# An S4 convolution and gMLP kernel on one core: constant matmuls put into the opening of TensorE's stream

## The chip, the core and the metric

The kernel runs on one core of one Trainium2 chip. A core has five engines with instruction streams of their own: TensorE (matmuls out of SBUF into PSUM; its weight loads are shown as a stream of their own, PEld), VectorE (DVE), ScalarE (ACT), GpSimd (POOL) and SyncE (SP, which here only starts transfers). The metric is the device time in microseconds, as a median over runs; lower is better.

## What is computed

One block with two halves, each behind a layer norm whose shift and scale come from a conditioning vector. The first half is a diagonal state space model with complex poles, applied as a long convolution over 2048 positions; the second is a gated MLP with a 2048 × 2048 matrix over positions. All inputs and outputs are float32.

```
mod = (silu(c) @ w_mod) -> sa, ca, ga, sb, cb, gb          # 576 -> 6 x 576
h = layernorm(x) * (1 + ca) + sa
  dt = exp(log_dt);  P = exp(dt * A * l), l = 0..2047
  K = real(sum_n C * P * dt * B)                            # 576 x 2048, 128 poles a channel
  y = irfft(rfft(h) * rfft(K)) + h * Dskip
x = x + ga * y
h = layernorm(x) * (1 + cb) + sb
  z = gelu(h @ w_in);  z1, z2 = halves;  z2 = layernorm(z2)
  g = w_sp @ z2 + b_sp
x = x + gb * ((z1 * g) @ w_out)
```

## The kernel before

The change lies in the function `ssm`, which does the first half; the MLP, which takes the greater part of the time, is not touched.

The order of the work in `ssm` is written out by hand. `ORDER` is a long string of steps; each is a letter and a number, and the letter names a generator function. At each mention of a step the generator runs on to its next `yield`, so the pieces of one unit are spread between those of others. Every instruction is pinned: each engine executes its instructions in the order in which the program issues them, and waits in place for what an instruction needs. Buffers in SBUF and PSUM are taken from rings whose order is written out too (`PLAN`); in PSUM `pk` has four banks of 512 float32 columns and `ps` two pairs of banks.

The steps that the change or the prediction touches:

- `O` and `P` (`poles`): VectorE and ScalarE turn the poles' inputs into exponents and phases, split each into three bfloat16 parts and store them in DRAM (through POOL's queue). `O` is for the first quarter of the channels, `P` for the rest.
- `M0` to `M5` (`mod_unit`): one sixth of w_mod each. TensorE multiplies the six row chunks of a half (288 columns) by silu(c) (`ec`), four chunks side by side in 32 array columns each, into bank `pm[0]` for the first half and `pm[1]` for the second. ScalarE copies both into `mpart`; the step's next piece sums the four row groups with a matmul by `ones` ("row sum") into two further banks. M2 comes first (it gives `gar`, the gate), then M1 (`cga`), M0 (`sga`), and later M3 to M5. M2's products are the first work of TensorE in the program.
- `e` (`e_unit`), `t` (`t_unit`), `p` (`p_unit`): for each of 36 groups of channels the poles' exponentials (ScalarE) and their sines and cosines, from phases that TensorE makes by bfloat16 products with selection matrices (`sel`), and the products of both (VectorE).
- `k` (`kg_unit`, the pole unit): contracts over the 128 poles on TensorE, in small tiles, into the first 256 columns of one bank; ScalarE copies them to `kab`.
- `1` (`k1_unit`): the first stage of the transform of the filter, from `kab` into the first 256 columns of two banks.
- `S`, `R`, `A` (`ln_stats`, `ln_rows`, `ln_half`): the layer norm, and the first stage of the transform of the rows, sixteen `A` units of two row blocks and 288 channels each, into four banks, 64 partitions for each block.
- `u`, `z`, `v`, `y`: the further stages of the transform, the multiplication in the frequency domain, and the way back.

`small` is a tile of constants in SBUF, 7 × 128 float32 columns; `eye`, its first 128 columns, is the unit matrix. `halfpi` is a column of the tile `consts_s`, which VectorE fills at the program's start; `bc(ap, shape)` broadcasts a column without a copy. `HC` is 288. The products of M, of the row sums and of the A units fill 288 of 512 columns, those of the k and 1 units 256.

The helper that records every instruction is line 224, so nearly all rows of the profile have this line; they are told apart by tiles.

Of the kernel before, what the change touches and what calls it, by code (L numbers as in the profile page):

```python
# [48 lines left out]
    "zz": "01011010010100010110100110101101010101",  # L49
}  # L50
ON_ACT = set()
PE_SUMS = set(range(28, 36))
PE_ADDS = set(range(8, 20))
ORDER = """
# [182 lines left out]
def ssm(tc, I, x1_d, consts_s, dram, mod_d, mlp):  # L237
# [3 lines left out]
    HC = 288  # L241
    ring = Rings()
    CW = 16 * 9 * 128
    with ExitStack() as ctx:
# [10 lines left out]
        def ps2():  # L255
            return ring(psp, [128, 2, 512], F32, "ps", 2)

        def ps1():
            return ring(psp, [128, 512], F32, "pk", 4)
# [175 lines left out]
        gsp = ep.tile([128, D], BF, name="gsp", bufs=1)  # L435
        msk = cp.tile([128, 2], F32, name="msk")

        def mod_unit(k):
            wm = wmt.pop(k)
            pm = [ps1(), ps1()]  # L440
            for hh in range(2):
                for kt in range(6):
                    j = (kt + 2 * hh) % 4
                    T.matmul(pm[hh][32 * j:32 * j + 32, :HC], ec[:, kt:kt + 1].to_broadcast([96, 32]),
                             wm[hh][:, kt], start=kt < 4, stop=kt >= 2, skip_group_check=True)
            yield
            mpart = ep.tile([128, D], F32, name="mpart", bufs=1)
            for hh in range(2):
                A.activation(v3(mpart)[:, hh], pm[hh][:, :HC], AF.Copy)
            yield  # L450
            pm = [ps1(), ps1()]
            for hh in range(2):
                T.matmul(pm[hh][:, :HC], ones, mpart[:, HC * hh:HC * hh + HC], start=True, stop=True)
            yield
            src = [t[:, :HC] for t in pm]
            if k == 2:
                for hh in range(2):
                    A.activation(v3(gar)[:, hh], src[hh], AF.Copy)
            elif k == 1:
                for hh in range(2):  # L460
                    V.scalar_tensor_tensor(v3(cga)[:, hh], src[hh], 1.0, v3(gar)[:, hh], op0=ALU.add, op1=ALU.mult)
            elif k == 0:
                for hh in range(2):
                    V.tensor_tensor(v3(sga)[:, hh], src[hh], v3(gar)[:, hh], op=ALU.mult)
                yield
                for i in range(2):
                    A.activation(gsp, sga, AF.Copy)
                    yield
                    V.scalar_tensor_tensor(sga, gsp, msk[:, i:i + 1], sga, op0=ALU.mult, op1=ALU.add)
                    yield  # L470
                A.activation(gsp, sga, AF.Copy)
            else:
                mrow = mpart if k == 4 else ep.tile([128, D], F32, name="gar", bufs=1)
                for hh in range(2):
                    if k == 4:
                        A.activation(v3(mrow)[:, hh], src[hh], AF.Identity, bias=one)
                    else:
                        A.activation(v3(mrow)[:, hh], src[hh], AF.Copy)
                yield
                G.dma_start(mod_d[k - 3:k - 2], mrow[0:1])  # L480
# [59 lines left out]
        def ln_half(k):  # L540
            p, h = divmod(k, 2)
            c = slice(HC * h, HC * h + HC)
            pms = [ps1() for _ in range(4)]
            for t in range(2):
                n, rt, cs = row[2 * p + t]
                for x, y, st in ((cs, gsp, True), (rt, n, False)):
                    for g in range(4):
                        rows = slice(32 * g, 32 * g + 32)
                        T.matmul(pms[g][64 * t:64 * t + 64, :HC], x[rows], y[rows, c], start=st, stop=not st, skip_group_check=True)
                yield  # L550
            o = ring(ep, [128, 4, HC], F32, "st1o", 2)
            for g, pm in enumerate(pms):
                A.activation(o[:, g], pm[:, :HC], AF.Copy)
                yield
            G.dma_start(u1_d[:, 2 * p:2 * p + 2, :, :, c].rearrange("g b r k d -> (b r k) g d"), o)
# [22 lines left out]
        def t_unit(g):  # L578
            c, gi = divmod(g, 9)
            pa = ps2()  # L580

            def phases(cols, start, stop):
                for k, (n, c0) in enumerate(zip(("lc", "la"), cols)):
                    for h, (l, r) in enumerate(zip(halves(lt[n, c], gi), rows(c0, 256))):
                        T.matmul(pa[:, h].rearrange("p (c k j) -> p k c j", c=8, k=2)[:, k], l, r, start=start, stop=stop, skip_group_check=True)

            def magics(c0, start):
                for h, (l, r) in enumerate(zip(rows(c0, 128), rows(2048, 64))):
                    T.matmul(pa[:, h].rearrange("p (c j) -> p c j", c=8), l, r[:, None, :].to_broadcast([48, 8, 64]), start=start, stop=False,
                             skip_group_check=True)  # L590

            if g in ROUNDED:
                magics(2112, True)
                phases((768, 0), False, False)
                magics(2240, False)
                phases((1536, 1792), False, True)
                yield
                cs = tt[g] = ring(tb, [128, 2, 2, 512], F32, "ft", 3)
                ct, f = cs[:, 0], cs[:, 1]
                if g in ON_ACT:  # L600
                    A.activation(ct, pa, AF.Abs)
                else:
                    V.tensor_single_scalar(ct.bitcast(I32), pa.bitcast(I32), 0x7FFFFFFF, op=ALU.bitwise_and)
                yield
                A.activation(f, pa, AF.Sin, scale=-TWO_PI)
            else:
                phases((768, 0), True, True)
                yield
                cs = tt[g] = ring(tb, [128, 2, 2, 512], F32, "ft", 3)
                ct, f = cs[:, 0], cs[:, 1]  # L610
                A.activation(f, pa, AF.Copy, bias=MAGIC)
                yield
                V.scalar_tensor_tensor(f, f, MAGIC, pa, op0=ALU.subtract, op1=ALU.subtract)
                yield
                V.tensor_single_scalar(ct.bitcast(I32), f.bitcast(I32), 0x7FFFFFFF, op=ALU.bitwise_and)
                yield
                A.activation(f, f, AF.Sin, scale=-TWO_PI)
            yield
            A.activation(ct, ct, AF.Sin, bias=halfpi, scale=-TWO_PI)
# [17 lines left out]
        def kg_unit(g):  # L637
            pr, pi, gr, gi = tt.pop(g)
            pm = ps1()
            for j in range(4):  # L640
                rows = slice(32 * j, 32 * j + 32)
                T.matmul(pm[rows, 63:256:64], eye[:, rows], dsk[:, 4 * g:4 * g + 4], start=True, stop=False, skip_group_check=True)
            for i in range(4):
                for x_, y_, sp in ((gr, pr, False), (gi, pi, True)):
                    for j in range(4):
                        c = 8 * (j // 2) + 2 * i + j % 2
                        T.matmul(pm[32 * j:32 * j + 32, 64 * i:64 * i + 64], x_[:, c], y_[:, c].rearrange("p s j -> p (s j)"),
                                 start=False, stop=sp, skip_group_check=True)
            yield
            kk = kab[g] = ring(tb, [128, 4, 64], F32, "kab", 2)  # L650
            A.activation(kk, pm[:, :256].rearrange("p (i b) -> p i b", i=4), AF.Copy)

        def k1_unit(g):
            c, gi = divmod(g, 8)
            kk = kab.pop(g)
            pm = [ps1(), ps1()]
            for i in range(4):
                for ri in range(2):
                    for h in range(2):
                        s = slice(64 * h, 64 * h + 64)  # L660
                        T.matmul(pm[h][64 * ri:64 * ri + 64, 64 * i:64 * i + 64], kk[s, i], r1[ri][s, s], start=True, stop=True,
                                 skip_group_check=True)
            yield
            if c not in k1t:
                k1t[c] = ring(kp, [128, 32, 128], F32, "k1", 2)
            o = k1t[c][:, :, 16 * gi:16 * gi + 16].rearrange("p k (h c) -> p k h c", h=2)
            for h in range(2):
                pk = pm[h][:, :256].rearrange("p (c k) -> p k c", c=8)
                if (g, h) in COPIED:
                    V.tensor_copy(o[:, :, h], pk)  # L670
                else:
                    A.activation(o[:, :, h], pk, AF.Copy)
                yield
# [1794 lines left out]
```

## Time and profile before

| | |
|---|---|
| median of 3 runs | 1692.17 us (1691.11 to 1693.82) |
| the profiled execution | 1691.0 us, its span 1688.9 us |
| TensorE busy | 1615.6 us, 16868 matmuls |
| VectorE, ScalarE, GpSimd busy | 1298.4, 873.8, 209.7 us |
| mean granted TensorE clock | 0.99 |
| first matmul | 25.77 us after the span's start |

A page of the profile gives busy times by engine, the span in 40 slices, the DMA queues, the chain of work that ended last, and groups of instructions. A row of the timeline starts with the time and the duration in microseconds, then the engine, the operation, "out<-in", the shapes (for a matmul the array's rows*columns, then the moving operand) and the number of merged records (x12); in brackets stand the idle time of the engine before it and what ended this. A row of busy times gives the stretch, its length, busy time and number of instructions of each engine, the granted TensorE clock (1.00 is full), the DMA engines' busy share and GB/s. A row of waits gives who waited for whom, the sum in microseconds, the number of waits and the longest.

### The profile page before, as it was taken

To read this page: it belongs to the slowest core of one execution; us is meant where nothing else is said; L and a number is where in the kernel's file an instruction comes from. 1 tells how busy PE (TensorE), PEld (TensorE's weight loads), DVE (VectorE), ACT (ScalarE), POOL (GpSimd) and SP (SyncE) were. 2 spreads that over 40 slices of the span, in tenths; PEclk is the share of its full clock that TensorE was granted. 3 is DMA by queue.
4 is the path that set the end of the run, shared out by engine and by line. 5 is a ranking of instruction groups with operands and counts; after the bars stand their busy time and mean duration, and the time that the engine had idled before them with its cause. 6 is when DMAs were issued, how large, how long until landed. Compare 5 with 4: busy or idle time off the path is not lost.

```text
span 1688.9 us, 39922 instructions
## 1 busy us (share of the span) xinstructions
PE 1615.6 (96%) x16868; PEld 1235.7 (73%) x16868; DVE 1298.4 (77%) x2241; ACT 873.8 (52%) x1307; POOL 209.7 (12%) x340
## 2 busy tenths in 40 slices
PE   3778999989999999999999999999999999999999
PEld 1344677755555557778878888888888888888887
DVE  7898999867989877988997776894443487787555
ACT  6889999675776664555444433342321133353221
POOL 3251111112222110000000000000111100111100
PEclk9978999999999999999999999999999999999999
DMA  9667645596888898776738887664667573777560
GB/s 231 170 215 229 203 140 176 171 317 208 280 287 243 251 261 297 242 270 234 249 118 302 282 292 257 219 218 166 232 213 243 189 221 121 275 281 252 189 241 29
DMA packets 186402, 380.61 MB, mean 225 GB/s; under 512 B 38464, under 2 KB 105792, under 8 KB 185456
## 3 DMA queue, kind: packets, MB, share of 16 engines
q1 hardware_dynamic: 145216, 182.10, 35.2%
q0 software_dynamic: 34528, 169.11, 30.1%
q10 hardware_dynamic: 6480, 26.86, 3.9%
q8 instruction: 132, 2.16, 0.5%
q14 instruction: 46, 0.38, 0.1%
HBM read 272.73 MB, written 105.29 MB: 224 GB/s over the span
## 4 chain that ended last, share of the span: by engine, by line
PE 77%; DVE 7%; DMA 3%; issue 2%; ACT 2%; SPq 0%; POOL 0%; ACTq 0%; DVEq 0%; POOLq 0%
PE ps L224 58%; PE pz L224 10%; PE pk_b L224 2%; PE pk_a L224 2%; DMA zset<-set_d 2%; PE pk_c L224 2%; PE pk_d L224 1%; DVE zset L224 1%; DVE gt L224 1%; DVE bsz L224 1%; PE ps_a L224 0%; PE ps_b L224 0%; DMA v_d<-v_a 0%; PE pt L224 0%; DMA uu_a<-in_x 0%
## 5 line engine op out<-in xcount | busy, mean ns | idle before, releaser
L224 PEld LDWEIGHTS <-zset 128*128 128x128 f16 x7182 | 702.2, 98 | 86.5 <-DMA zset<-set_d 2.0
L224 PE MATMUL ps<-wsp,zset 128*128 128x256 f16 x6048 | 666.8, 273 | 2.2 <-DMA zset<-set_d 1.1
L224 PE MATMUL pz<-wz,nt 128*128 128x512 f16 (+1 forms) x1120 | 220.8, 358 | 1.5 <-ACT nt L224 1.0
L224 ACT ACTIVATE z<-gt 128x1024 f16<-128x1024 f32 x56 | 59.0, 1054 | 250.4 <-DVE gt L224 250.4
L224 PEld LDWEIGHTS <-nt 128*128 128x128 f16 x1120 | 109.4, 98 | 107.1 <-ACT nt L224 1.5
L2164 POOL DMA_DIRECT2D zset<-set_d x96 | 50.8, 529 | 862.5 <-PE ps L224 619.7
L224 PE MATMUL ps<-wout,z 128*128 128x288 f16 x1092 | 138.4, 286 | 0.0
L224 DVE SCALAR_TENSOR_TENSOR gt<-ps,sc,bsp 128x512 f32<-128x512 f32 x36 | 27.0, 749 | 143.0 <-PE ps L224 141.3
L224 PEld LDWEIGHTS <-z 128*128 128x128 f16 x1176 | 115.1, 98 | 28.9
L224 DVE TENSOR_TENSOR raw<-raw 128x256 f32<-128x256 f32 (+3 forms) x238 | 126.8, 539 | 7.7 <-DMA raw<-z_d 3.5
L224 PE MATMUL ps<-n2o,zset 128*128 128x256 f16 x1134 | 128.2, 273 | 0.0
L224 DVE SCALAR_TENSOR_TENSOR gt<-ps,sc,gt 128x512 f32<-128x512 f32 (+1 forms) x180 | 122.2, 696 | 7.6
L224 ACT ACTIVATE zset<-raw 128x1792 f16<-128x1792 f32 x48 | 81.1, 1691 | 59.3 <-PE ps L224 21.6
L224 DVE TENSOR_TENSOR zset<-raw,zset 128x1792 f16<-128x1792 f32 x48 | 96.9, 2020 | 15.7 <-ACT zset L224 15.7
L224 DVE TENSOR_TENSOR z<-ps,z 128x512 f32<-128x512 f32 (+1 forms) x126 | 72.0, 599 | 32.3 <-ACT z L224 25.9
L224 ACT ACTIVATE z<-pz,sc 128x512 f32<-128x512 f32 (+1 forms) x96 | 51.9, 574 | 39.9 <-PE pz L224 32.7
L224 ACT ACTIVATE wsp<-raw,sc 128x1792 f16<-128x1792 f32 x25 | 44.5, 1783 | 46.2 <-DVE raw L224 40.2
L224 ACT ACTIVATE z<-z,sc 128x1024 f32<-128x1024 f32 x21 | 24.1, 1148 | 76.0 <-DVE z L224 72.3
L224 ACT ACTIVATE z1b<-gt 128x512 f16<-128x512 f32 (+1 forms) x22 | 17.7, 821 | 84.0 <-DVE gt L224 84.0
L224 PE MATMUL ps<-n2q,wf 128*128 128x512 f16 x252 | 55.7, 379 | 0.0
L224 DVE BATCH_NORM_STATS2 bsz<-z 128x6 f32<-128x384 f32 x96 | 48.4, 548 | 5.0 <-ACT z L224 4.4
L224 DVE SCALAR_TENSOR_TENSOR wsp<-raw,sc,wsp 128x1792 f16<-128x1792 f32 x25 | 52.0, 2078 | 0.3 <-ACT wsp L224 0.3
(793 smaller groups left out, 2772.0 us busy)
## 6 DMA issues: line engine op xcount, KB each, us to landing
zset<-set_d POOLq DMA_DIRECT2D x96, 896.0 KB, 5.2
raw<-z_d SPq DMA_DIRECT2D x48, 512.0 KB, 5.6
set_d<-zset ACTq DMA_DIRECT2D x24, 896.0 KB, 6.4
z_d<-z POOLq DMA_DIRECT2D x32, 576.0 KB, 8.2
zset<-wa_d POOLq DMA_DIRECT2D x18, 896.0 KB, 4.9
raw<-in_w_spT SPq DMA_DIRECT2D x25, 512.0 KB, 4.4
set_d<-zset SPq DMA_DIRECT2D x12, 896.0 KB, 5.8
wst<-in_w_in SPq DMA_DIRECT2D x8, 1024.0 KB, 9.3
```

What stands on the lines that cost most here:

```text
L224: return self.tc.keep_in_program_order(f(*a, **k))
L2164: self.nc.gpsimd.dma_start(o, self.set_d[f, j - 1] if j else self.wa_d[f])
```

## The change

A new helper `warm(t, n, c0, const)` issues n float32 matmuls into the columns of the PSUM tile t from c0 to the bank's end, which no instruction reads. Their weights are the unit matrix and their moving operand columns of `small` (or, for M2, the constant column `halfpi`, broadcast to both). It is called

- in `mod_unit` ahead of the first half's products and again between the halves, with the two numbers that `WARM_M` gives for each of the six steps, and three times behind the row sums;
- in `ln_half` three times behind the second row block;
- in `t_unit` eight times ahead of the phases of group 1, over all 512 columns;
- in `kg_unit` three times behind groups 0 to 9, and in `k1_unit` three times behind groups 0 to 8.

```
@@ -49,6 +49,7 @@
     "zz": "01011010010100010110100110101101010101",
 }
 ON_ACT = set()
+WARM_M = {0: (5, 10), 1: (12, 14), 2: (116, 8), 3: (0, 3), 4: (0, 3), 5: (0, 3)}
 PE_SUMS = set(range(28, 36))
 PE_ADDS = set(range(8, 20))
 ORDER = """
@@ -435,10 +436,20 @@
         gsp = ep.tile([128, D], BF, name="gsp", bufs=1)
         msk = cp.tile([128, 2], F32, name="msk")
 
+        wide = small.rearrange("p i c -> p (i c)")
+
+        def warm(t, n, c0, const=None):
+            for _ in range(n):
+                l, r = (eye, wide[:, c0:]) if const is None else (bc(const, [128, 128]), bc(const, [128, 512 - c0]))
+                T.matmul(t[:, c0:], l, r[:, :512 - c0], start=True, stop=True, skip_group_check=True)
+
         def mod_unit(k):
             wm = wmt.pop(k)
             pm = [ps1(), ps1()]
+            warm(pm[0], WARM_M[k][0], HC, halfpi if k == 2 else None)
             for hh in range(2):
+                if hh:
+                    warm(pm[0], WARM_M[k][1], HC, halfpi if k == 2 else None)
                 for kt in range(6):
                     j = (kt + 2 * hh) % 4
                     T.matmul(pm[hh][32 * j:32 * j + 32, :HC], ec[:, kt:kt + 1].to_broadcast([96, 32]),
@@ -451,6 +462,7 @@
             pm = [ps1(), ps1()]
             for hh in range(2):
                 T.matmul(pm[hh][:, :HC], ones, mpart[:, HC * hh:HC * hh + HC], start=True, stop=True)
+            warm(pm[1], 3, HC)
             yield
             src = [t[:, :HC] for t in pm]
             if k == 2:
@@ -547,6 +559,8 @@
                     for g in range(4):
                         rows = slice(32 * g, 32 * g + 32)
                         T.matmul(pms[g][64 * t:64 * t + 64, :HC], x[rows], y[rows, c], start=st, stop=not st, skip_group_check=True)
+                if t:
+                    warm(pms[3], 3, HC)
                 yield
             o = ring(ep, [128, 4, HC], F32, "st1o", 2)
             for g, pm in enumerate(pms):
@@ -578,6 +592,8 @@
         def t_unit(g):
             c, gi = divmod(g, 9)
             pa = ps2()
+            if g == 1:
+                warm(pa[:, 0], 8, 0)
 
             def phases(cols, start, stop):
                 for k, (n, c0) in enumerate(zip(("lc", "la"), cols)):
@@ -646,6 +662,7 @@
                         c = 8 * (j // 2) + 2 * i + j % 2
                         T.matmul(pm[32 * j:32 * j + 32, 64 * i:64 * i + 64], x_[:, c], y_[:, c].rearrange("p s j -> p (s j)"),
                                  start=False, stop=sp, skip_group_check=True)
+            warm(pm, 3 if g < 10 else 0, 256)
             yield
             kk = kab[g] = ring(tb, [128, 4, 64], F32, "kab", 2)
             A.activation(kk, pm[:, :256].rearrange("p (i b) -> p i b", i=4), AF.Copy)
@@ -660,6 +677,7 @@
                         s = slice(64 * h, 64 * h + 64)
                         T.matmul(pm[h][64 * ri:64 * ri + 64, 64 * i:64 * i + 64], kk[s, i], r1[ri][s, s], start=True, stop=True,
                                  skip_group_check=True)
+            warm(pm[1], 3 if g < 9 else 0, 256)
             yield
             if c not in k1t:
                 k1t[c] = ring(kp, [128, 32, 128], F32, "k1", 2)
```

More of the change, by code (lines that the diff above doesn't have):

```diff
@@ L51 @@
 ON_ACT = set()
+WARM_M = {0: (5, 10), 1: (12, 14), 2: (116, 8), 3: (0, 3), 4: (0, 3), 5: (0, 3)}
 PE_SUMS = set(range(28, 36))
@@ L436, in ssm, with warm @@
         msk = cp.tile([128, 2], F32, name="msk")
+        wide = small.rearrange("p i c -> p (i c)")
+        def warm(t, n, c0, const=None):
+            for _ in range(n):
+                l, r = (eye, wide[:, c0:]) if const is None else (bc(const, [128, 128]), bc(const, [128, 512 - c0]))
+                T.matmul(t[:, c0:], l, r[:, :512 - c0], start=True, stop=True, skip_group_check=True)
         def mod_unit(k):
@@ L440, in mod_unit @@
             pm = [ps1(), ps1()]
+            warm(pm[0], WARM_M[k][0], HC, halfpi if k == 2 else None)
             for hh in range(2):
+                if hh:
+                    warm(pm[0], WARM_M[k][1], HC, halfpi if k == 2 else None)
                 for kt in range(6):
@@ L453, in mod_unit @@
                 T.matmul(pm[hh][:, :HC], ones, mpart[:, HC * hh:HC * hh + HC], start=True, stop=True)
+            warm(pm[1], 3, HC)
             yield
@@ L549, in ln_half @@
                         T.matmul(pms[g][64 * t:64 * t + 64, :HC], x[rows], y[rows, c], start=st, stop=not st, skip_group_check=True)
+                if t:
+                    warm(pms[3], 3, HC)
                 yield
@@ L580, in t_unit @@
             pa = ps2()
+            if g == 1:
+                warm(pa[:, 0], 8, 0)
             def phases(cols, start, stop):
@@ L648, in kg_unit @@
                                  start=False, stop=sp, skip_group_check=True)
+            warm(pm, 3 if g < 10 else 0, 256)
             yield
@@ L662, in k1_unit @@
                                  skip_group_check=True)
+            warm(pm[1], 3 if g < 9 else 0, 256)
             yield
```

## The prediction

> **What bounds the kernel now.** I read the page first (engines, slices, chain), then busy times by stretch, then the instructions of the opening in order of time.
>
> ```profile
> PE 1615.6 (96%) x16868; PEld 1235.7 (73%) x16868; DVE 1298.4 (77%) x2241; ACT 873.8 (52%) x1307; POOL 209.7 (12%) x340
> PE   3778999989999999999999999999999999999999
> PEclk9978999999999999999999999999999999999999
> PE 77%; DVE 7%; DMA 3%; issue 2%; ACT 2%; SPq 0%; POOL 0%; ACTq 0%; DVEq 0%; POOLq 0%
> ```
>
> TensorE (PE) is busy 1615.6 of 1688.9 us and makes up 77% of the chain that ended last; only the first four slices (42 us each) leave it room, and only there is the clock row below 9. So the account is TensorE's: everything put into its stream has to find a hole, and the holes are early. The stretches say how large they are.
>
> ```profile
> core 0: us, PE busy (x) PEld busy (x) DVE busy (x) ACT busy (x) POOL busy (x), PEclk, DMA share, GB/s
> 0.00:160.00 160.00, 106.90 (x1944) 54.30 (x1946) 134.67 (x276) 134.10 (x258) 57.91 (x96) 0.89 0.73 209
> 160.00:400.00 240.00, 226.30 (x4512) 162.07 (x4508) 208.36 (x305) 197.97 (x340) 41.65 (x66) 1.00 0.70 206
> 400.00:1688.90 1288.90, 1282.40 (x10419) 1019.34 (x10416) 955.41 (x1662) 541.71 (x710) 110.17 (x178) 1.00 0.70 231
> ...
> 25.70:50.60 24.90, 21.64 (x108) 8.26 (x111) 16.38 (x33) 16.55 (x25) 7.83 (x15) 1.00 1.02 256
> ...
> 77.90:84.70 6.80, 5.70 (x64) 2.65 (x71) 6.77 (x12) 6.79 (x15) 0.97 (x2) 0.50 0.55 188
> ...
> 88.50:94.50 6.00, 5.76 (x134) 3.67 (x133) 5.61 (x11) 5.40 (x10) 4.69 (x8) 0.50 0.90 320
> ...
> 98.60:108.70 10.10, 7.73 (x138) 3.95 (x134) 8.23 (x20) 8.96 (x18) 5.28 (x9) 0.51 0.72 215
> ...
> 139.60:149.80 10.20, 8.44 (x96) 3.21 (x94) 7.48 (x11) 9.16 (x17) 2.81 (x4) 0.52 0.39 141
> ```
>
> The columns after the times are busy us (and instructions) of each engine, the granted clock, the DMA share and GB/s. After 160 us TensorE idles 240 − 226.3 + 1288.9 − 1282.4 = 20.2 us in all, so nothing that is late at 160 us is made good later. Before 160 us it idles 53.1 us, 25.8 of them before its first instruction. Four stretches ran at half clock. A fifth did too, though its clock column says 1.00 (no change of clock had been recorded yet): the same group of products takes 2.13 us at 25.77 and 0.92 us at 51.99, the same sum 1.12 us (37.67 to 38.79) and 0.58 us (54.17 to 54.75).
>
> ```profile
> 25.77 2.13 PE L224 MATMUL pk_a<-wm,ec 96*32 96x288 f32 x12 [25.77 <-DVE t_q L224]
> ...
> 37.67 1.33 PE L224 MATMUL pk_a<-mpart,small 128*128 128x288 f32 x2
> 38.79 1.17 PE L224 MATMUL pk_b<-mpart,small 128*128 128x288 f32 x2
> ...
> 51.99 0.92 PE L224 MATMUL pk_c<-wm,ec 96*32 96x288 f32 x10
> ...
> 54.17 0.65 PE L224 MATMUL pk_b<-mpart,small 128*128 128x288 f32 x2
> 54.75 0.39 PE L224 MATMUL ps_b<-sel,lb 48*128 48x512 bf16 x2
> ```
>
> **The change, part by part.** Nothing is removed or moved; TensorE gets matmuls whose results nobody reads ("fillers"), all f32, 128 rows by 128 columns of weights. I count them from the diff. With 224 moving columns: M0 15, M1 26, M2 124, M3 to M5 9, the six row sums 18, sixteen row units (A) 48: together 240. With 256: ten pole units (k) 30 and nine k1 units (1) 27: 57. With 512: the second phase unit (t1) 8.
>
> *Price of one.* An f32 matmul is two records: one half of a w_mod group is six matmuls in the code and x12 in the row at 25.77, and one row sum is one matmul and x2. How long a record holds the array when equal ones follow each other stands in the v units' rows.
>
> ```profile
> 170.75 0.19 PEld L224 LDWEIGHTS pk_d<-zz_a,small 64*128 64x128 f32 x1
> 170.75 0.38 PE L224 MATMUL pk_d<-zz_a,small 64*128 64x256 f32 x1
> 170.97 0.37 PE L224 MATMUL pk_d<-zz_a,small 64*128 64x256 f32 x1
> 171.19 0.38 PE L224 MATMUL pk_d<-zz_a,small 64*128 64x256 f32 x1
> 171.40 0.38 PE L224 MATMUL pk_d<-zz_a,small 64*128 64x256 f32 x1
> ...
> L224 PEld LDWEIGHTS pk_b<-xb_b,small x2: 186/188/189, 327.3 to 327.4; 128*128 128x128 f32 x2
> ...
> 327.31 1.13 PE L224 MATMUL pk_b<-xb_b,small 128*128 128x512 f32 x2
> 328.36 0.32 PE L224 MATMUL pk_b<-u_b,st 128*64 128x128 f32 x1
> ```
>
> From 170.75 to 171.40 three steps take 0.65 us: 0.217 us for 256 columns, 0.85 ns a column, weight loads hidden. For 224 columns that is 0.19 us, just the 0.188 us that a load of 128 f32 columns takes, so 0.38 to 0.39 us a filler in a long run. Where a group stands alone, its first load shows: the 512-column matmul takes 1.05 us (327.31 to 328.36) against 2 × 512 × 0.85 ns = 0.87, the row sum 0.58 against 0.49. So each of the 51 groups gets 0.15 us on top. Sum: 240 × 0.39 = 93.6; 57 × 2 × 0.217 = 24.7; 8 × 0.87 = 7.0; 51 × 0.15 = 7.6; together 133 us. Lower end: 0.38 and no edges, 123 us. Upper end: the row sum's 0.58 us scaled by columns (0.45, 0.52, and 1.05 for the wide ones), 108 + 29.6 + 8.4 = 146 us. I take 133, because 116 of the fillers stand in one run, as the v rows do.
>
> *The front run of M2.* M2's products are TensorE's first work, and wait until 25.77 us; the fillers before them read only a constant that VectorE sets in the first microsecond.
>
> ```profile
> 0.82 0.06 DVE L185 MEMSET consts_s<- 128x1 f32 x1 [0.82 <-PEq L2457]
> ...
> PE pk_a L224 <- DVE t_q L224: 25.8, 1, 25.8
> ...
> 27.94 0.41 ACT L224 ACTIVATE mpart<-pk_a 128x288 f32<-128x288 f32 x1 [1.63 <-PE pk_a L224]
> ...
> DVE ft_c L224 <- PE ps_a L224: 4.5, 1, 4.5
> ```
>
> They start at 0.95 us and 116 × 0.39 = 45.2 us follow, some of it at half clock. From a low clock to a high one the trace shows stretches with 5.70 us (77.9) to 21.64 us (25.7) of work; half of that is lost: 2.9 to 10.8 us. The fillers are dense, so I take 2.9. M2's products then begin at 0.95 + 45.2 + 2.9 = 49 us instead of 25.77. The hole takes in 25 us; the other 24 are on the path. Late next is ScalarE: its mpart copy, 27.94 now, comes after 49, and the exponentials and splits of the poles that follow it on ScalarE wait, and VectorE for those. POOL's stores of these splits are late with them.
>
> The Trainium skill ("TensorE: Matmul & The Clock Gate", section "The HAM clock gate") says that the clock rises after about 3.4 us of sustained work and falls after an idle window of that length. By it the front run would lose 1.7 us and not 2.9, an estimate, and the total would be 1 us lower. The trace agrees only in part: the stretch at 25.7 stayed slow for 24.9 us with 21.64 us busy, at 96- and 48-row matmuls between 128-row ones.
>
> *What the clock gives back.*
>
> ```profile
> 50.60:77.90 27.30, 20.36 (x414) 10.34 (x407) 26.65 (x52) 26.42 (x54) 8.73 (x14) 1.00 0.52 129
> ...
> 108.70:139.60 30.90, 23.00 (x634) 13.48 (x624) 30.06 (x56) 28.33 (x56) 13.17 (x21) 0.99 0.73 237
> ```
>
> The five slow stretches hold 21.64 + 5.70 + 5.76 + 7.73 + 8.44 = 49.3 us of TensorE work; at full clock 24.6 us less. Bounds: zero (they stay slow) to 24.6. I take 23: with fillers behind nearly every unit the array hardly rests, and these two stretches kept the clock with the array busy three quarters of the time.
>
> *Idle time.* From 25.77 to 160 us TensorE idles 160 − 25.8 − 106.9 = 27.3 us, in short pieces; the largest sum of one kind after the first wait is this:
>
> ```profile
> PE pk_a L224 <- ACT st1o_b L224: 2.4, 2, 1.8
> ```
>
> Fillers stand where these pieces are, and the work of VectorE and ScalarE (134.7 and 134.1 us) has more time than before. I leave 6 of it (0 to 27.3).
>
> *The copies behind a filler.* ScalarE's copies of a unit's PSUM tile may have to wait for the three fillers on the same bank (0 to 1.3 us each). While TensorE is the bound this is hidden by TensorE's own next units; without that cover it lengthens the k–1 chain and the row units, 35 copies by 1.3, 46 us, and is not added to the same time twice.
>
> *Sum.* The point at which 160 us stood comes to 0.95 + 2.9 + (106.9 − 23) + 133 + 6 = 226.8 us, 66.8 later. What follows is full and stays as it is. The profiled execution took 1691.0 us for a span of 1688.9 (2.1 around it): 1688.9 + 66.8 + 2.1 = 1757.8. The median shown is 1.2 us above that execution, a spread that counts for nothing here; I say 1758.
>
> **The rivals.**
> 1. *A filler costs half.* If a constant product were one record (0.19 us), or the two ran side by side, the front run would end at 0.95 + 22.6 + 2.9 = 26.5, right where M2 waits now, and the total would be about 67 us: 0.95 + 2.9 + 83.9 + 67 + 6 = 160.8, 1693 us. It decides at 66 us of added TensorE time in all: below that the regained clock wins and the kernel is faster; with no idle left, 154.8, 1687 us. For it: the whole hole before M2 would be filled exactly. Against it: every f32 matmul with 128 weight columns in the trace has its two records, and the pitch of 0.217 us is per record.
> 2. *Loads not hidden.* With full 128-row weights a load may not go under the matmul of the same rows; the 512-column matmul showed 0.18 us for its two. At 0.39 + 0.18 = 0.57 us: 240 × 0.57 + 57 × 0.61 + 8 × 1.05 = 180 us, and the kernel comes to 1688.9 + 2.1 + 0.95 + 2.9 + 83.9 + 180 + 6 − 160 = 1805 us. Against it: v's 64-row loads, 0.19 us each, hide completely.
> 3. *The clock stays low.* If the dense f32 stream does not raise the clock sooner than the first stretch did, 10.8 us are lost in place of 2.9, and if only half of the 23 comes back, 12 more: 1778 us. For it: 21.64 us of work were needed once.
> 4. *The lateness is made good.* The 20.2 us of idle time after 160 us are used up, because VectorE and ScalarE are ahead by then: 1738 us. Against it: 8.9 us of them lie in 340 to 400, where VectorE is idle too and so not what TensorE waits for:
>
> ```profile
> 340.00:360.00 20.00, 16.69 (x202) 13.54 (x198) 14.45 (x34) 14.74 (x25) 3.29 (x6) 1.00 1.08 335
> 360.00:380.00 20.00, 16.07 (x146) 8.96 (x144) 13.79 (x34) 12.81 (x16) 4.26 (x7) 1.00 1.08 300
> 380.00:400.00 20.00, 18.32 (x129) 9.97 (x129) 9.89 (x22) 8.37 (x16) 6.31 (x9) 1.00 0.78 235
> ```
>
> **How the numbers follow.** Main case 0.68, with its own range 1740 to 1785 (123 us, idle 0 and all 24.6 back at the low end, 146 us and idle 20 at the high end); rival 1 0.08; rival 2 0.11; rival 3 0.08; rival 4 0.05. The range 1732 to 1800 takes in the main case, 3 and 4, and leaves out 1 and most of 2: 0.81. Two tenths of a per cent (3.4 us; the runs shown spread over 2.7) is what a measurement can tell from no change. Of rival 1, 0.04 ends faster, 0.03 within and 0.01 slower; everything else is slower: 0.93.
>
> **What would show it.** Right: first product of M2 near 49 us; fillers in pairs of records, 0.19 us apart; the granted clock full from some 5 us to 230; TensorE busy about 1615.6 + 133 + 3 − 23 = 1729 us; VectorE waiting 20 us or more for ScalarE or TensorE between 28 and 60; the part from u, z and v units on unchanged in length. Wrong: M2 still near 26 us (rival 1), records 0.28 us apart (rival 2), filler durations twice as long after the first 6 us (rival 3). A step of the sum that could fail unseen is the 6 us of idle time, if the units then wait for each other in turn.

## The result, and the profile after

The changed kernel takes 1760.14 us (median of 6 runs, 1753.82 to 1761.28) beside 1693.38 us of the kernel before (6 runs, 1691.11 to 1698.82): a ratio of 1.038 by the record's estimate, 95% interval 1.0362 to 1.0397 (the quotient of the two medians is 1.0394). The profiled execution took 1757.55 us for a span of 1755.6, 66.7 us more than the span before. The kernel is slower, by about the amount forecast (1758); two of the prediction's readings behind that number did not hold, and the experiments show which.

The page of the changed kernel, the lines that answer to those shown of before:

```profile
PE 1729.4 (99%) x17478; PEld 1344.0 (77%) x17478; DVE 1299.6 (74%) x2241; ACT 875.8 (50%) x1307; POOL 210.4 (12%) x340
PE   9999999998999999999999999999999999999999
PEclk9999999999999999999999999999999999999999
PE 83%; DVE 7%; DMA 4%; ACT 3%; issue 2%; POOL 0%; ACTq 0%; SPq 0%; DVEq 0%; POOLq 0%
```

TensorE has 610 matmul records more, two for each of the 305 fillers, and is busy 113.8 us longer. Its first slices are full now, and the clock row shows no slice below 9. The other engines do what they did before.

The start of TensorE's stream, from the timeline of the changed kernel:

```profile
0.94 47.10 PE L225 MATMUL pk_a<-consts_s 128*128 128x224 f32 x232 [0.94 <-DVE consts_s L188]
47.97 1.16 PE L225 MATMUL pk_a<-wm,ec 96*32 96x288 f32 x12
49.06 3.32 PE L225 MATMUL pk_a<-consts_s 128*128 128x224 f32 x16
...
66.03 4.70 PE L225 MATMUL pk_c<-small 128*128 128x224 f32 x24
```

The front run of 116 fillers (232 records) lasts 47.03 us, so M2's first products begin at 47.97 us and not at 25.77. They take 1.16 us there and not 2.13: the array is at full speed by then. The second group shows the pitch of a run: its 24 records start 0.189 us apart, 0.38 us a filler.

Busy times of the changed kernel in 10-us stretches of the front run (columns as in the prediction):

```profile
0.00:10.00 10.00, 9.06 (x34) 8.56 (x35) 6.30 (x27) 4.12 (x7) 0.21 (x4) 1.00 0.65 169
10.00:20.00 10.00, 10.00 (x55) 9.92 (x54) 6.71 (x26) 8.73 (x22) 5.41 (x9) 1.00 0.99 308
...
40.00:50.00 10.00, 10.00 (x60) 8.96 (x59) 0.00 (x0) 0.00 (x0) 0.00 (x0) 1.00 0.54 173
```

The first row holds 34 records and the second 55 (one that reaches into two stretches counts in both). The single records start 0.373 us apart up to 6 us and 0.191 us apart after that. At the later pace the 232 would take 44.3 us, so 2.7 us of the 47.03 were lost to a slow start of some 5.2 us. The clock column says 1.00 in that row too, as it did in the prediction's slow first stretch, and is not to be trusted there. In a second execution of the same kernel (after_again, below) the pace changes at 3.7 us already, M2 starts at 46.83 us, and 1.6 us are lost; over all the runs that have a front run it changes between 3.7 and 6.7 us. The Trainium skill ("TensorE: Matmul & The Clock Gate", section "The HAM clock gate") gives about 3.4 us of sustained work until the clock rises; the prediction's estimate from it, 1.7 us lost, is too low for the first execution and fits the second.

From 40 to 50 us neither VectorE nor ScalarE did anything at all. The waits of the changed kernel up to 235 us name what they waited for:

```profile
ACT mpart L225 <- PE pk_a L225: 33.7, 3, 26.9
...
DVE ft_a L225 <- PE ps_a L225: 28.7, 2, 28.1
```

The fillers alone, by groups, in the first 230 us (busy us, then mean ns of one record, then idle time before them); shown are those of M2 and the four groups with 256 columns, which are those of the k and 1 units:

```profile
L225 PE MATMUL pk_a<-consts_s 128*128 128x224 f32 x248 | 50.4, 366 | 0.9 <-DVE consts_s L188 0.9
...
L225 PE MATMUL pk_a<-small 128*128 128x256 f32 x42 | 10.9, 396 | 0.0
L225 PE MATMUL pk_d<-small 128*128 128x256 f32 x36 | 9.4, 396 | 0.0
...
L225 PE MATMUL pk_b<-small 128*128 128x256 f32 x24 | 6.2, 396 | 0.0
...
L225 PE MATMUL pk_c<-small 128*128 128x256 f32 x12 | 3.1, 396 | 0.0
```

All ten groups, 610 records, add up to 139 us. The means of 366 and 396 ns are the length of one record from its start to its modelled end; successive records overlap, and the pitch is half of that. The groups also overlap with each other and with the work records beside them: up to the mark named below the fillers' records cover 137 us, and without them TensorE would be busy 130 us less.

To see when the delay arises, the opening needs a mark that both kernels have: ScalarE's first copy `uu_a`, which opens the stages behind the fillers. For the kernel before, then for the changed one:

```profile
L224 ACT ACTIVATE uu_a<-pk_d x3: 597/598/613, 159.4 to 313.0; 128x512 f32<-128x512 f32 x3
```

```profile
L225 ACT ACTIVATE uu_a<-pk_d x3: 597/597/654, 221.2 to 373.5; 128x512 f32<-128x512 f32 x3
```

It comes 61.8 us later (159.4 to 221.2). The busy times up to this mark give the whole account; the kernel before, then the changed one:

```profile
0.00:159.40 159.40, 106.30 (x1940) 53.96 (x1940) 134.07 (x275) 133.50 (x257) 57.91 (x96) 0.89 0.73 208
```

```profile
0.00:221.20 221.20, 215.93 (x2544) 160.05 (x2544) 135.49 (x276) 134.72 (x258) 57.98 (x96) 0.99 0.53 154
```

TensorE's idle time fell from 53.1 to 5.3 us, of which 0.94 lie ahead of its first record. Its busy time rose by 109.6 us: 130 of fillers, less 20 by which its other records cover less at the higher clock (106.3 us before, 86.1 now). If time in which a filler and another record overlap is counted as the filler's, it is 137 less 28. 109.6 − 47.8 = 61.8.

The remaining 5 us of the 66.7 come behind the openings, in the MLP. From `uu_a<-pk_b` (381.4 us before, 441.9 after) to the end of the span it is 1307.5 us before and 1313.7 after; between the two copies 1.3 us were won. The rows of the long products in the kernel before and the changed one, cut to that part:

```profile
L224 PE MATMUL ps<-wsp,zset 128*128 128x256 f16 x6048 | 666.8, 273 | 2.2 <-DMA zset<-set_d 1.1 <-DVE zset L224 0.9
```

```profile
L225 PE MATMUL ps<-wsp,zset 128*128 128x256 f16 x6048 | 668.9, 273 | 6.6 <-DMA zset<-set_d 3.8 <-DVE zset L225 2.7
```

TensorE waits 4.4 us longer for `zset`, for its transfers and for VectorE. In another profile of the changed kernel the same part took 1312.4 us, in one experiment (noK) 1312.3, in all others 1307 to 1309. So it isn't one odd execution; what makes these transfers late stays open.

### The profile page after: what moved, and what is told of

Read it like the earlier page. It is cut to its first block, busy times and chain, and to the rows that moved or that the text cites. A ratio compares the mean times of both kernels' runs of the same rounds, so it can differ in the third digit from the quotient of the medians.

```text
span 1755.6 us, 41142 instructions
## 1 busy us (share of the span) xinstructions
PE 1729.4 (99%) x17478; PEld 1344.0 (77%) x17478; DVE 1299.6 (74%) x2241; ACT 875.8 (50%) x1307; POOL 210.4 (12%) x340
## 4 chain that ended last, share of the span: by engine, by line
PE 83%; DVE 7%; DMA 4%; ACT 3%; issue 2%; POOL 0%; ACTq 0%; SPq 0%; DVEq 0%; POOLq 0%
PE ps L225 52%; PE pz L225 12%; PE pk_a L225 7%; PE pk_b L225 4%; PE pk_c L225 3%; PE pk_d L225 3%; DMA zset<-set_d 2%; DVE zset L225 1%; PE ps_a L225 1%; DVE gt L225 1%; DVE raw L225 1%; DMA v_d<-v_a 1%; PE ps_b L225 1%; PE pt L225 1%; DVE ot L225 0%
## 5 line engine op out<-in xcount | busy, mean ns | idle before, releaser
L225 DVE TENSOR_TENSOR zset<-raw,zset 128x1792 f16<-128x1792 f32 x48 | 97.0, 2020 | 17.3 <-ACT zset L225 17.3
```

Of the source, the lines that this page charges most:

```text
L225: return self.tc.keep_in_program_order(f(*a, **k))
```

## The experiments

The theory of the prediction: behind the hole before M2, TensorE is the bound of the opening, so that every filler counts with its whole time, less what the clock gives back and a few us of idle time. The rivals that remained: a filler that costs half would make the kernel faster (rival 1, which "decides at 66 us of added TensorE time in all"); or the fillers cost little where they stand among waits, and a few places carry the whole loss.

Medians are over runs, marks and rows from one profiled execution of each kernel. Those of a kernel differ by some us (the kernel before: 1691.0 us profiled, 1691.21 to 1705.36 in one set of runs), and the two profiles of the changed kernel by 2.1 us at the mark, so a difference of that size between two marks tells nothing.

### What the front run costs

The kernel front116 keeps only the 116 fillers ahead of M2's products; nofront leaves out only these.

```
front116:  WARM_M = {0: (0, 0), 1: (0, 0), 2: (116, 0), 3: (0, 0), 4: (0, 0), 5: (0, 0)}
           # and no other warm(...) call
nofront:   WARM_M = {0: (5, 10), 1: (12, 14), 2: (0, 8), 3: (0, 3), 4: (0, 3), 5: (0, 3)}
```

> Only the 116 fillers ahead of M2's products stay, all other fillers are out. My account: they run from 0.95 to about 48 us and M2 starts at 48 in place of 25.77; what followed at half clock up to 50.6 then runs at full clock (21.64 us of work, 10.8 less), but ScalarE and VectorE, which stood still meanwhile, have to catch up. Expected 12 to 20 us over the kernel before: 1704 to 1712. If lateness at the start were made good later: no more than 3 us over. If the whole loss came from the front run: 1760.

> All fillers but the 116 ahead of M2. Left are 189 of the 305, worth 133 - 45 = 88 us by my price, and the hole before M2 stays empty. Expected: 25.8 + 2.9 + 83.9 + 88 + 6 = 206.6 us at the point that was 160, so 46 us over the kernel before, about 1739. If the front run made the whole loss: about 1692 or faster, as the clock is kept up.

Measured beside a median of 1695.99 us for the kernel before: front116 1716.22 us, ratio 1.0117 (1.0099 to 1.0134); nofront 1738.75 us, ratio 1.0252 (1.0234 to 1.027). The two losses, 20.2 and 42.8 us, add up to 63.0; the changed kernel loses 62.2 (1758.28 beside 1696.04, below). So the two parts add up to the whole here, and the front run is a third of the loss. It is just above the 12 to 20 us expected; nofront is close to its 46. Up to the mark, front116:

```profile
0.00:182.50 182.50, 151.15 (x2170) 102.30 (x2172) 135.12 (x276) 133.56 (x257) 58.12 (x96) 0.83 0.65 186
```

and nofront:

```profile
0.00:202.00 202.00, 170.49 (x2312) 115.25 (x2312) 135.63 (x276) 135.06 (x258) 57.78 (x96) 1.00 0.58 168
```

The mark comes 23.1 us late in front116, near the 22.4 us by which M2 starts later (48.20 us). But this lateness was not handed on as it was. ScalarE's copy `kab_a`, at 108.95 us before, is only 14.5 us late:

```profile
123.49 0.38 ACT L225 ACTIVATE kab_a<-pk_a 128x256 f32<-128x256 f32 x1 [0.34 <-PE pk_a L225]
```

Some 8 us were made good in the first stretch behind M2, which now ran at full clock, and were lost again later. In the profiled execution the span is 24.9 us longer; by the medians the loss is 20.2, since the kernel before ran at 1695.99 us in these runs, 5 us above its profiled execution. The mean clock of 0.83 up to the mark can't be set beside the 0.89 of before, whose column counts the slow stretch up to 50.6 us as full. Behind these stretches, before and in front116:

```profile
50.60:159.40 108.80, 84.66 (x1838) 45.70 (x1830) 99.84 (x181) 100.79 (x198) 41.20 (x64) 0.84 0.64 194
```

```profile
57.70:182.50 124.80, 96.43 (x1856) 52.51 (x1857) 104.50 (x187) 108.69 (x209) 41.25 (x64) 0.75 0.59 174
```

The front run keeps the clock up for some ten us beyond its end; from there on it is lower than before. In nofront the column shows a full clock, and the idle time, 31.5 us, is the hole before M2 and 6 us beside it.

### The row units' fillers, and the changed kernel once more

noA leaves out the 48 fillers behind the row units; after_again is the changed kernel, run beside it.

```
noA:
-                if t:
-                    warm(pms[3], 3, HC)
```

> The changed kernel without the three fillers behind each of the sixteen row units: 48 of 305 out, 48 x 0.38 = 18 us of array time and sixteen first loads. If TensorE is the bound of the opening from end to end, as my sum has it, every microsecond taken out shows: 18 to 21 us faster than the changed kernel, 43 to 48 us over the kernel before. If the copies that wait behind the fillers cost on top (up to 1.2 us on each of sixteen): up to 38 us faster. If the idle time comes back: less than 12.

> The changed kernel once more, for its trace. In its first trace the opening was 62 us later than before and the span 66.7; the other 5 us arose behind 440 us, where TensorE waited for transfers of zset. If those 5 us were that execution's alone, the part behind the opening is now within 2 us of the 1307.5 us that the kernel before has from the copy into uu_a at 381.4 to its end; if they belong to the change, again 1312 or more.

Measured beside 1696.04 us of the kernel before: noA 1756.92 us, ratio 1.037 (1.0346 to 1.0394); after_again 1758.28 us, ratio 1.0377 (1.0355 to 1.0399). Leaving out 18 us and more of fillers (48 × 0.38) gained 1.4 us, which the intervals don't tell from nothing: the expectation's case that the idle time comes back. Up to its mark, at 222.5 us, noA shows:

```profile
0.00:222.50 222.50, 205.21 (x2448) 146.48 (x2448) 135.69 (x276) 135.02 (x258) 57.70 (x96) 0.93 0.53 152
```

Busy time fell by 10.7 us, and idle time rose by 12.0, from 5.3 to 17.3. The clock went with it, 0.99 to 0.93, which is why 18 us of fillers are only 10.7 us of busy time: the rest of the work got longer. One stretch with row units shows both, in the changed kernel and in noA:

```profile
120.00:130.00 10.00, 8.83 (x91) 4.99 (x88) 7.98 (x21) 9.34 (x20) 1.55 (x2) 0.83 0.38 127
```

```profile
120.00:130.00 10.00, 7.79 (x94) 3.28 (x93) 9.01 (x22) 9.97 (x20) 2.30 (x3) 0.66 0.38 129
```

ScalarE is busy 9.97 of 10 us without the fillers: it bounds this stretch, by its copies out of PSUM, for which TensorE's next units wait. The waits of noA from 100 to 230 us:

```profile
PE pk_a L225 <- ACT st1o_b L225: 3.2, 2, 1.8
PE pk_c L225 <- ACT st1o_b L225: 2.7, 3, 1.4
```

In the changed kernel no wait of TensorE for `st1o` is longer than 0.3 us. Here the 48 fillers filled time in which TensorE would have waited, and cost next to nothing. That contradicts the prediction's reading that behind the hole each us of fillers is on the path.

The fall of the clock in noA needed no long idle stretch: no wait of TensorE between 100 and 230 us is longer than 1.8 us, and from 117 to 126 us the array was busy 1.59, 1.73 and 2.25 of 3 us, at mean clocks of 1.00, 0.72 and 0.50. The Trainium skill ("TensorE: Matmul & The Clock Gate", section "The HAM clock gate") ties the fall to an idle window of about 3.4 us; here the clock fell with the array busy more than half of the time.

### The pole units' fillers

noK leaves out the 57 fillers behind the k and 1 units and keeps all others.

```
noK:
-            warm(pm, 3 if g < 10 else 0, 256)        # kg_unit
-            warm(pm[1], 3 if g < 9 else 0, 256)      # k1_unit
```

> The changed kernel without the fillers behind the k units and the 1 units; those of the front, of the row sums and of the row units (ln_half) stay. 57 fillers x 0.38 us + 19 edges x 0.15 us = 24 us of TensorE time goes. In the changed kernel the lag behind the kernel before grows by about 15 us between 108 us and 165 us of the kernel before's time, where the k and 1 units lie, and by next to nothing in the row units ahead of them. Theory A, the k and 1 fillers stand in front of work that is waited for: the time falls by 12 to 25 us, to 1733 to 1746, and the lag stays near 45 us from 108 us on. Theory B, the clock and the idle time take it back as they did when the row units' fillers were left out: within 4 us of 1758, and the granted clock in the stretch from 170 to 230 us falls.

Measured beside 1696.18 us of the kernel before: 1744.46 us, ratio 1.0279 (1.026 to 1.0298). That is 13.8 us below the changed kernel, 16.6 by the ratios: theory A, near its low end. Up to its mark, at 207.7 us:

```profile
0.00:207.70 207.70, 194.12 (x2436) 142.82 (x2436) 134.53 (x275) 134.09 (x258) 57.75 (x96) 0.98 0.55 161
```

Busy time fell by 21.8 us, idle time rose by 8.3, so 13.5 us were won up to the mark. How the gain arises is seen at ScalarE's copies of the pole units, which the two kernels share; one of them in the kernel before, the changed kernel and noK:

```profile
108.95 0.38 ACT L224 ACTIVATE kab_a<-pk_a 128x256 f32<-128x256 f32 x1
```

```profile
156.09 0.39 ACT L225 ACTIVATE kab_a<-pk_a 128x256 f32<-128x256 f32 x1 [1.58 <-PE pk_a L225]
```

```profile
149.43 0.39 ACT L225 ACTIVATE kab_a<-pk_a 128x256 f32<-128x256 f32 x1
```

The changed kernel is 47.1 us late at this copy, and ScalarE waits 1.58 us for the bank, just as long as the six records of fillers take that stand between the unit's products and this copy:

```profile
154.49 1.56 PE L225 MATMUL pk_a<-small 128*128 128x256 f32 x6
```

noK is 40.5 us late and does not wait. My expectation put the whole difference behind 108 us. That was wrong in the place: at this copy half of it (6.6 us, or 4.8 beside the second profile of the changed kernel) is there already, and it grows to 13.5 us at the mark. Nor does noK's lag stay near 45 us: it is 48.3 at the mark and 55.1 at the end. The fillers of the k and 1 units stand between a unit's products and the copy that the next step waits for, and there they cost about half of their 29.6 us (the four rows of 256 columns above). The price is uncertain by some us, since noK has two TensorE waits without a named cause, 2.5 us at 153 us and 2.6 at 210, that the changed kernel has not.

### Fewer fillers in front

front56 has 56 fillers ahead of M2's products and no others, so that the hole is filled to the point and M2 starts where it did.

```
front56:   WARM_M = {0: (0, 0), 1: (0, 0), 2: (56, 0), 3: (0, 0), 4: (0, 0), 5: (0, 0)}
           # and no other warm(...) call
```

> Only 56 fillers ahead of M2's products, nothing else. At 0.385 us each and 2.9 us for the slow start they end at 25.4 us, so M2 is on time and starts at full clock. My account: the stretch from 25.7 to 50.6 holds up to 10.8 us less TensorE work, of which VectorE's wait of 4.5 us for the first phases shows that at least some is on the path: 4 to 8 us faster, 1684 to 1688. If VectorE and ScalarE alone bound the opening: within 2 us of the kernel before.

Measured: 1694.71 us beside 1695.99, ratio 0.9989 (0.9978 to 0.9999). M2 starts at 25.60 us with a warm array:

```profile
25.60 0.69 PE L225 MATMUL pk_a<-wm,ec 96*32 96x288 f32 x8 [0.23 <-DMA wm<-in_w_mod]
```

Eight of its twelve records are in this row; their pitch is the fast one. VectorE's step of the layer norm that was at 50.39 us before is at 45.73: 4.7 us were really won, and at ScalarE's copy `kab_a` 4.5 us are still there (104.50 beside 108.95). By 116 us 0.1 us is left. The expected 4 to 8 us did not come; 1.3 us by the medians is what the other case, within 2 us, said. TensorE's waits up to 160 us begin with these:

```profile
PE ps_a L225 <- DMA la<-pa_d: 5.2, 2, 2.8
PE pk_c L225 <- issue: 4.1, 1, 4.1
```

The first lies between 30 and 37 us, ahead of the 4.7 us that were won: TensorE is early for the phases, whose split has to come back from DRAM. The second is what took the lead: TensorE stands from 106.0 to 110.1 us for nothing that the trace names; the longest such wait in the kernel before is 0.6 us up to its mark.

The records of the DMA queues say more of it. Over all twelve traces TensorE has 22 waits of 1 us and more without a named cause in the first 250 us, none of them in the kernel before or the changed one. All but one end 2.2 to 3.0 us after a packet of 16 KB has started on an instruction queue, though these packets come only every 7 us on the median (3.3 at the least). So TensorE most likely waited for its own instructions. Why the transfer came too late at these places is not shown.

### Cheaper fillers, to test rival 1

In bf16fill all 305 fillers stay, but as bfloat16 products, one record each in place of two; bf16ak has these only behind the row, k and 1 units; front128b has only a front run of them, 128 with 384 columns, made to end where M2 can start.

```
bf16fill, bf16ak, front128b (warm):
-                l, r = (eye, wide[:, c0:]) if const is None else (bc(const, [128, 128]), bc(const, [128, 512 - c0]))
+                l = (eye if const is None else one).bitcast(BF)
+                l, r = (l[:, :128], l) if const is None else (bc(l[:, :1], [128, 128]), bc(l[:, :1], [128, 512 - c0]))
+                r = bc(l[:, :1], [128, 512]) if c0 == 0 else r
bf16ak:     WARM_M all (0, 0); no warm behind the row sums and in t_unit
front128b:  WARM_M 2: (128, 0), all others (0, 0); warm from column 128; no other warm(...) call
```

> The same 305 fillers in the same places, read as bfloat16 (the same bytes, seen as 16-bit numbers): one record each and one column a step, by the bf16 rows of the MLP (0.110 us for 256 columns) 0.10 us each, 35 us in all instead of 133. That is below the 66 us at which I said the change turns. My account: the front run ends near 14 us, M2 is on time, 23 us of fillers are put in behind it while the clock gives back up to 23 us; VectorE and ScalarE become the bound of the opening; 2 to 12 us faster than the kernel before, 1680 to 1690. If it is not the price but the presence of fillers in the stream (waits on the banks, order) that costs: 1720 or more.

> Of the 305 cheap (bfloat16) fillers only those behind the row, pole and k1 units, 105 in number, about 0.1 us each: 11 us and some first loads. The run with all cheap fillers lost 5 us up to 90 us, where the w_mod group and the first phases stand, and 7 more from 108 on. If a filler in front of waited-for work costs its time wherever it stands: 5 to 12 us over the kernel before. If only those in the chain of the w_mod units cost: within 3 us of it. If the clock they keep pays for them: 2 to 5 us faster.

> The front run alone, as 128 fillers of 384 columns read as bfloat16: 128 x 0.163 us and some 3 us for the slow start, so it ends near 25 us like the 56 f32 fillers did; but it adds 256 TensorE instructions (a load and a matmul each), where the 56 added 224. With the 56 the opening was 3.4 us ahead at 105 us, and then TensorE stood 4.1 us between two matmuls of one pole unit with no wait that the profile shows, at the time of a packet on the instruction queue, which moves 16.4 KB a packet, 256 instructions if each has 64 bytes. If it is the fetch of instructions: the borders lie now as in the kernel before, no wait over 1 us of this kind, and 3 to 5 us faster than before, 1690 to 1693 beside 1696. If the wait belongs to the transfers of that time: again a stop of 3 us or more near 105 us and no gain.

Measured: bf16fill 1703.31 us beside 1695.99, ratio 1.0046 (1.0032 to 1.0059); bf16ak 1700.24 beside 1696.04, ratio 1.003 (1.0011 to 1.0049); front128b 1693.6 beside 1696.04, ratio 1.000 (0.9986 to 1.0014). None is faster. The start of bf16fill and that of front128b:

```profile
0.97 14.23 PE L225 MATMUL pk_a<-consts_s 128*128 128x224 bf16 x116 [0.97 <-DVE consts_s L188]
25.42 1.19 PE L225 MATMUL pk_a<-wm,ec 96*32 96x288 f32 x8 [10.22 <-DMA wm<-in_w_mod]
```

```profile
0.97 23.76 PE L225 MATMUL pk_a<-consts_s 128*128 128x384 bf16 x128 [0.97 <-DVE consts_s L188]
```

In bf16fill the front run ends 10 us early, and the clock is down again when M2 comes (eight records take 1.19 us and not 0.69). Its later fillers are cheap, 0.12 us each in the front run's pace (14.23 us for 116), some 23 us for the other 189 at that pace; and still its mark lies at 171.0 us, 11.6 late. (The profiled execution, 1707.86 us, is the slowest of its twelve.) Up to the mark:

```profile
0.00:171.00 171.00, 138.16 (x2242) 80.56 (x2242) 134.64 (x275) 134.27 (x257) 57.92 (x96) 0.88 0.68 194
```

The clock column gives 0.88 and 0.89 before, but counts the slow start of the kernel before as full. Behind 50.6 us it is 0.90 beside 0.84, and TensorE's other 1940 records cover 99.8 us and not 106.3: the fillers did keep the clock up for a part. Of the 24 us that they added behind the hole 6.5 came back so and 5.7 by idle time used up; the remaining 12 us are the lateness. In the idle time that is left stands a wait of 3.1 us at 116 us without a named cause. bf16ak shows the same without any front run: 13.7 us added, 6.8 given back (99.5 us), no idle time used up, and the mark at 166.3 us, 6.9 late; its 4.2 us by the medians lie between the expectation's cases. Rival 1's point of decision was thus wrong as far as these fillers can stand for its own: with far less than 66 us of added time the kernel is still slower, because the clock gave back some 7 us and not 23.

In front128b the front run reaches up to M2, and no unnamed wait is over 1.2 us, about as expected if the instructions were what front56 waited for; the 3 to 5 us of gain that should have followed did not come (the medians differ by 2.4 us, which the interval does not tell from nothing). Its lead is 4.6 us at the copy that stood at 108.95 us before (104.35), and 0.7 us at the mark (158.7). From there to 162 us, the kernel before and front128b:

```profile
108.00:162.00 54.00, 43.08 (x1167) 25.47 (x1161) 47.40 (x78) 49.68 (x95) 17.43 (x27) 0.90 0.71 226
```

```profile
104.00:162.00 58.00, 46.24 (x1171) 26.02 (x1167) 48.46 (x79) 50.19 (x97) 17.66 (x28) 0.82 0.66 211
```

The same work takes 4 us longer, and the clock is lower, 0.82 for 0.90. So the clock was the suspect.

### Is it the clock that takes the lead away?

late3 adds to front128b three f32 fillers behind each of the row units 9 to 14, in that stretch.

```
late3 (ln_half):
+                if t and 9 <= k < 15:
+                    warm(pms[3], 3, HC)
```

> The kernel with 128 one-record fillers in front of w_mod's products (front128b) and, in addition, three two-record fillers behind the row units 9 to 14 of the opening, where front128b showed a granted clock of 0.70 to 0.82 between 104 and 150 us and lost its lead of 3 to 4.6 us. 18 fillers x 0.38 us = 7 us of TensorE time added. Theory A, they fill time in which TensorE waits and hold the clock up, so that the lead stays: 2 to 5 us faster than the kernel before, 1691 to 1694 beside 1696. Theory B, they stand in front of waited-for work: 1 to 7 us slower than the kernel before. Theory C, the lead is lost for another reason (the copies of VectorE and ScalarE bound that stretch): within 1.5 us of it.

Measured: 1699.3 us beside 1696.18, ratio 1.002 (1.0009 to 1.0032): slower by some 3 us, in the range of theory B, and theory A falls. The profiled execution is its fastest, 1693.51 us, so the rows show less than the whole loss. The same stretch:

```profile
104.00:162.00 58.00, 51.51 (x1223) 34.31 (x1217) 48.27 (x79) 49.84 (x95) 17.20 (x27) 0.91 0.67 212
```

The fillers did what they were put there for: the clock is 0.91 and not 0.82. The stretch is as long as without them all the same; the mark is at 159.1 us. So a higher clock bought with fillers did not keep the lead. ScalarE's rows show where front128b lost it. Two waits for TensorE's products, 2.0 us (1.0 before) and 1.0 (none before), took about 1 us each, and there the low clock may have had its part. Another 1.4 us went at a wait for the store of an earlier `st1o`, first the kernel before, then front128b:

```profile
ACT st1o_b L224 <- DMA u_d<-st1o_b: 1.0, 1, 1.0
```

```profile
ACT st1o_b L225 <- DMA u_d<-st1o_b: 2.4, 1, 2.4
```

In late3 ScalarE is still 1.9 us ahead at 157 us of the kernel before's time; the copy of the mark then comes 1.6 us later for a wait that the trace does not name. Why late3's median is higher than front128b's stays open.

## Why the prediction was right, and where it was not

Its total held: 1758 said, 1760.14 measured, and 1757.55 in the profiled execution beside 1757.8. Step by step:

- *Price of a filler.* 0.38 to 0.39 us forecast in a long run, two records each; 0.38 measured, and 610 records for 305 fillers. The sum over all, 133 us, was 130 to 137 by what the records cover up to the mark; well inside 123 to 146.
- *The front run.* M2 at 49 us forecast, 47.97 measured. Slow start 2.9 us forecast, 2.7 measured, and 1.6 in the second execution. Late next was ScalarE's `mpart` copy (a wait of 26.9 us) and then VectorE (28.1 us, where 20 or more were forecast). front116 gives the step a price of its own: 20.2 us, beside the 24 that the prediction put on the path; on the way it was down to 14.5.
- *What the clock gives back.* 23 us forecast, 20 to 28 measured, by how the overlap with fillers is counted. The sum that counts is TensorE's work up to the mark: 215.9 us measured, 2.9 + 133 + 83.9 = 219.8 forecast for a point 0.6 us further on.
- *Idle time left.* 6 us forecast, 4.3 measured.
- *The opening's lag.* 66.8 us forecast, 61.8 measured. The 5 us too much are some 3 us of TensorE's work and 2 us of idle time.
- *What follows stays as it is.* This step failed: the part behind the opening grew by some 5 us, in waits for `zset`. The two errors have opposite signs; without this luck the forecast would have been 5 us too high. TensorE busy 1729 us, as forecast, is right for the reason given, since waits don't count there.
- *After the hole every filler is on the path.* The sum was built as if each us of fillers moved the end by a us, less the clock. As a sum it holds only because all were put in at once. Taken one by one, 18 us of fillers behind the row units cost 1.4 us (noA), 29.6 us behind the k and 1 units 14 to 17 (noK), 47 us in front 20 (front116). Without the row units' fillers, waits for ScalarE's copies and a lower clock take their place (noA); without the others a part of it comes back as idle time. So the idle time that was left (6 us forecast, 4.3 measured) was nearly right, and said nothing on what a single filler costs.
- *Copies behind a filler.* Costed at nothing, under TensorE's own next units. For the row units that is so; at the pole units ScalarE waits for the bank (1.58 us at 156.09). That part of noK's gain lies there is likely; no run separates it.
- *Rivals.* 1: records were not halved, and where the experiments made them cheap, the turning point of 66 us did not hold. bf16fill loses where the prediction said that regained clock would win: the clock gave back 6.5 us and not 23. 2: no; loads were hidden, at a pitch of 0.19 us a record. 3: no; the clock was up after some 6 us. 4: no; nothing of the lag was made good behind the opening.

## What to carry to other kernels

Price work put into an engine's idle gaps by two numbers: its duration times its count, and what the gap's owner does. Where another engine's copies bound a stretch, work taken out can be worth next to nothing (noA), and clock gained by fillers too (late3, which ended 0.2% slower). Where the added work stands between a product and the copy that the next step waits for, it costs about half (noK). A hole at the start is only free up to its end: 116 fillers overran it by 22 us and cost 20, and even those that fit it exactly gained next to nothing (0.1% in front56, none that shows in front128b). A lead of 4 us won early can be lost to causes that have nothing to do with the change's purpose, here a wait that goes with instruction transfers and one for a store. Compare lags at several marks: at the last one alone front116 would seem to hand its delay on unchanged.

## What the runs showed of the hardware

- The slow start of a dense stream of 128-row f32 matmuls (records 0.373 us apart and not 0.191) lasted until 6.1 us in one execution and 3.7 in another of the same kernel, and cost 2.7 and 1.6 us. The clock column showed 1.00 in it; the starts of like records show it, the column doesn't, so means of that column can't be compared across it.
- The mean granted clock was 0.66 in a stretch in which TensorE was busy 7.79 of 10 us and never waited over 1.8 us at a time (noA), and 0.83 with 8.83 busy (the changed kernel).
- TensorE waits with no cause in the trace, 4.1 us in front56, 3.1 and 2.6 in bf16fill, 2.5 and 2.6 in noK, 2.4 in bf16ak at 114 us, end 2.2 to 2.7 us after a 16-KB packet on an instruction queue has started. That speaks for the fetch of TensorE's instructions; front128b, made to tell, has none over 1.2 us but did not get faster.
- A bfloat16 filler of 224 columns took 0.12 us where the f32 one took 0.41 (the front runs, slow start included in both): more than the factor of two in records.
